# A fused hash-attention and cosine feed-forward kernel: two products issued behind the output copies, one AV step moved, the last tile in two halves, and a new prologue

## The chip, the cores and the metric

The kernel runs on one core of a Trainium2 chip. The metric is device microseconds of one execution, the median over runs; the profile is one such run, and its span is about 1.8 us shorter than that run's time. A ratio is the mean time of one kernel's fast runs over that of the other's of the same rounds, so it is not quite the ratio of the medians quoted beside it. The kernel before is run again beside each group of kernels: its medians were 312.5, 312.7, 312.6, 312.9, 312.9 and 312.4 us, with single runs from 311.8 to 315.4. (The fifth figure is the fourth's runs and one more.)

## The reference

```python
# q, k, v: [4, 8, 768, 64]; proj: [64, 6]; w_in: [512, 2048]; w_out: [2048, 512]
q_bits = (q @ proj > 0);  k_bits = (k @ proj > 0)      # 6 bits per token
mask   = bucket(q_bits)[..., :, None] == bucket(k_bits)[..., None, :]
scores = where(mask, q @ k.T / 8, -1e9)
x      = softmax(scores) @ v                           # -> [3072, 512]
h      = x @ w_in
out    = (h * cos(h)) @ w_out
```

The kernel puts the equality of buckets into the product itself: each token's six hash bits, scaled, are six further rows of q and k, so the score of a matching pair is raised and one exponential with a bias does the rest.

## The kernel before

Four batches of eight heads. The hash matmuls give the bits; the scores, the exponential and the AV product follow per head. When a batch's attention is done, its first feed-forward product (called L1, sixteen blocks of 128 columns with a cosine and a product h\*cos(h) each) runs as one stage in the next batch's attention; the second product (L2) fills PE between scores. There are four L1 stages; the attention stretches between them are called A2, A3 and A4 here. The instruction order on each engine is the program's own.

The L1 block, the output tile of L2 and the loop that joins them:

```python
def l1_ff(b, ff, hp):
    ...                                   # 8 matmuls into hp
    for c_, g_, h_ in pieces:
        nc.scalar.activation(out=c_, in_=h_, func=ACTF.Sin, bias=cos_bias, scale=1.0)
    for c_, g_, h_ in pieces:
        nc.vector.tensor_tensor(out=g_, in0=h_, in1=c_, op=ALU.mult)

def l2_mm():
    ...                                   # one matmul of 512 columns into m_ps
    if ff == NFF - 1:
        ob = obp.tile([P, D_MODEL], FP32, name="ob")
        ...
        if b == B - 1 and qt == T - 1:    # last tile: copied and stored in halves
            ...
        else:
            nc.vector.tensor_copy(out=ob, in_=o_ps)
            nc.sync.dma_start(out=dst, in_=ob)

for ff in range(NFF):                     # one L1 stage
    ...
    l1_ff(bb, ff, hp)
    ...                                   # for batch 0: a mark and loads
    if ff in (0, 1) and len(pend) > 0:
        av_step()
    if bb > 0:
        fill(L1F(ff))                     # L2 matmuls of the batch before
```

From the sixth pair of heads on, POOL issues the three loads of a pair (natq, natk, natv, 384 KB each). SP issues the transposes, and then four small transfers of bit rows per pair:

```python
def bits_dma(pr, js):                     # js = 0..3: q and k of head 0, q and k of head 1
    for j in js:
        dst = (qx(pr), kx(pr))[j % 2]
        nc.sync.dma_start(out=dst[D:KEXT, j // 2, :], in_=bits[pr][...])
```

PE's first score of a head waits for that head's two bit rows.

The softmax here doesn't subtract the row's maximum and nothing guards it: scores larger than these inputs give would overflow.

Of the kernel before, what the change touches and what calls it, by code (L numbers as in the profile page):

```python
# [9 lines left out]
FP32 = mybir.dt.float32  # L10
# [12 lines left out]
def kernel(  # L23
# [29 lines left out]
    NEARLY = 5  # L53

# [23 lines left out]
    wz = glob.tile([P, 512], FP16, name="wz")  # L78
    proj2 = glob.tile([32, 2, NBITS], FP32, name="proj2")
# [12 lines left out]
    state = {"m": 0, "rot": 0, "hold": False}  # L92
# [50 lines left out]
    def blocks(pr, hh=None):  # L143
        if pr not in blk:
            blk[pr] = [blkp.tile([P, 2, T, 2, 32], FP32, name=nm) for nm in ("blkq", "blkk")]
        for w in range(2):
            if hh is None:
                nc.vector.transpose(  # L148
                    out=blk[pr][w].rearrange("p h t c r -> p (h t c r)"),
                    in_=nat[pr][w].rearrange("p h f -> p (h f)"))  # L150
            else:
                nc.vector.transpose(
                    out=blk[pr][w][:, hh].rearrange("p t c r -> p (t c r)"),
                    in_=nat[pr][w][:, hh])
# [158 lines left out]
    def l1_ff(b, ff, hp):  # L313
        halves = hp if isinstance(hp, list) else [hp[:, c, :] for c in range(2)]
        for ft in range(NFT):
            for c in range(2):
                nc.tensor.matmul(  # L317
                    out=halves[c][:, 0:C2],
                    lhsT=win_t[ft][:, ff * P:(ff + 1) * P],
                    rhs=xT[(b, ft)][:, 3 * c:3 * c + 3, :],  # L320
                    start=(ft == 0), stop=(ft == NFT - 1))
        cos = cosp.tile([P, 2, C2], FP16, name="cos")
        g = gp.tile([P, 2, C2], FP16, name="g")
        if isinstance(hp, list):
            pieces = [(cos[:, c], g[:, c], halves[c][:, 0:C2]) for c in range(2)]
        else:
            pieces = [(cos, g, hp[:, :, 0:C2])]
        for c_, g_, h_ in pieces:
            nc.scalar.activation(out=c_, in_=h_, func=ACTF.Sin, bias=cos_bias, scale=1.0)  # L329
        for c_, g_, h_ in pieces:  # L330
            nc.vector.tensor_tensor(out=g_, in0=h_, in1=c_, op=ALU.mult)  # L331
        g_tiles[(b, ff)] = g

# [4 lines left out]

    def l2_mm():
        b, qt, ff = l2q.pop(0)  # L340
        if ff == 0 and not state["hold"]:
            state["m"] = 1 - state["m"]
        o_ps = m_ps[state["m"]]
        g = g_tiles[(b, ff)].rearrange("p c n -> p (c n)")
        nc.tensor.matmul(  # L345
            out=o_ps, lhsT=g[:, qt * P:(qt + 1) * P], rhs=wout_t[ff],
            start=(ff == 0), stop=(ff == NFF - 1))
        if ff == NFF - 1:
            ob = obp.tile([P, D_MODEL], FP32, name="ob")
            dst = out.rearrange("(b p t) n -> b t p n", b=B, t=T)[b, qt]  # L350
            if b == B - 1 and qt == T - 1:
                hw = D_MODEL // 2
                nc.vector.tensor_copy(out=ob[:, 0:hw], in_=o_ps[:, 0:hw])
                nc.sync.dma_start(out=dst[:, 0:hw], in_=ob[:, 0:hw])
                nc.vector.tensor_copy(out=ob[:, hw:], in_=o_ps[:, hw:])
                nc.scalar.dma_start(out=dst[:, hw:], in_=ob[:, hw:])
            else:
                nc.vector.tensor_copy(out=ob, in_=o_ps)  # L358
                nc.sync.dma_start(out=dst, in_=ob)

    def fill(n):
        for i in range(n):
            if l2q and not (state["hold"] and i > 0 and l2q[0][2] == 0):
                l2_mm()
# [17 lines left out]
    def warmup(n):  # L382
        for _ in range(n):
            nc.tensor.matmul(  # L384
                out=s_ps[1][:, 1, :], lhsT=wz[:, 0:P], rhs=wz, start=True, stop=True,
                skip_group_check=True)

    with tc.manual_schedule():
# [3 lines left out]
        nc.scalar.dma_start(out=proj2, in_=proj.rearrange("(c p) i -> p c i", c=2))  # L392
        nc.sync.dma_start(out=nat[0][0][:, 0], in_=aps[0][:, 0])
        nc.scalar.dma_start(out=nat[0][1][:, 0], in_=aps[1][:, 0])
        nc.sync.dma_start(out=nat[0][0][:, 1], in_=aps[0][:, 1])
# [4 lines left out]
        nc.vector.memset(wz, 0.0)  # L400
        nc.vector.memset(exp_bias, EXP_BIAS)
        nc.vector.memset(cos_bias, math.pi / 2.0)
        nc.vector.memset(projblk, 0.0)
# [14 lines left out]
        for b_ in range(4):  # L418
            nc.vector.tensor_copy(
                out=projblk[32 * b_:32 * b_ + 32, :, b_, 0:NBITS], in_=proj2)  # L420
        blocks(0, 0)
# [12 lines left out]
        rows_copy(nc.vector, pe_transposes(0, 0, 1, av_ps[0]))  # L434
        rows_copy(nc.scalar, pe_transposes(0, 0, 0, m_ps[0], range(0, 3)))
        rows_copy(nc.vector, pe_transposes(0, 0, 0, m_ps[1], range(3, 6)))
        blocks(0, 1)
# [66 lines left out]
        for u in range(U):  # L504
# [11 lines left out]
            if u in L1_AT:  # L516
                bb = L1_AT[u]
                state["hold"] = bb > 0
                for ff in range(NFF):
# [7 lines left out]
                    l1_ff(bb, ff, hp)  # L527
                    if bb == 0:
                        nc.gpsimd.tensor_copy(out=mark, in_=g_tiles[(0, ff)][:, 0, 0:1])
# [5 lines left out]
                    if ff in (0, 1) and len(pend) > 0:  # L535
                        av_step()
                    if bb > 0:
# [9 lines left out]
        for ff in range(NFF):  # L547
            hp = (s_ps[0], m_ps, s_ps[1])[ff % 3]
            l1_ff(B - 1, ff, hp)
# [32 lines left out]
```

## Time and profile before

| | before |
|---|---|
| time, median of 3 (range) | 312.45 us (312.0 to 312.58) |
| profiled span | 310.8 us, granted clock 0.999 |
| PE busy | 97% |
| A2, A3, A4 | 45.10, 44.90, 44.51 us |
| L1 stages one to four | 21.19, 25.41, 25.11, 20.80 us |
| end of the fourth stage to the end | 24.66 us |

A stage runs from its first to its last L1 matmul, and A2 to A4 are what lies between. Two lines of the page: the span, and the costliest group that waits for the output copy. A group's columns are line, engine, operation, tiles, count, then busy us and mean ns of one, then the idle time just before it and what ended most of that.

```profile
span 310.8 us, 7680 instructions
...
L345 PE MATMUL m_ps<-wout,g 128*128 128x512 f16 x384 | 109.1, 379 | 2.1 <-DVE ob L358 1.8
```

The view by windows over A2, A3 and A4; the columns are the window, its length, the busy us of PE, weight loads, DVE, ACT and POOL with counts, granted clock, DMA share and GB/s. PE leaves 0.3 us of A2 idle and next to nothing of the other two:

```profile
80.30:125.40 45.10, 44.79 (x523) 27.23 (x521) 37.33 (x90) 42.08 (x50) 28.72 (x41) 1.00 0.70 180
150.81:195.71 44.90, 44.84 (x524) 27.35 (x522) 35.43 (x91) 42.05 (x50) 24.36 (x33) 1.00 0.78 165
220.82:265.33 44.51, 44.51 (x463) 26.08 (x461) 23.57 (x62) 37.15 (x43) 2.89 (x4) 1.00 0.29 74
```

### The profile page before, as it was taken

How to read it: one execution, taken by the hardware profiler on the slowest of the kernel's cores; microseconds unless marked ns; L12 is line 12 of the kernel's file. 1: busy time of each engine (PE TensorE's matmuls, PEld its weight loads, DVE VectorE, ACT ScalarE, POOL GpSimd, SP SyncE). 2: the span in 40 equal slices, each digit the busy share in tenths (PEclk: the TensorE clock that was granted, in tenths of full speed). 3: DMA queues.
4: the chain of work that ended last, by engine and by line, in shares of the span. 5: the costliest groups of instructions: out<-in, count | busy, mean ns of one | idle time of the engine just before them, and what ended most of it. 6: DMA issues, size and time to landing. Idle time of an engine off the chain costs nothing.

```text
span 310.8 us, 7680 instructions
## 1 busy us (share of the span) xinstructions
PE 300.5 (97%) x3074; PEld 181.2 (58%) x3074; DVE 201.5 (65%) x434; ACT 234.1 (75%) x288; POOL 109.1 (35%) x180
## 2 busy tenths in 40 slices
PE   8899999899999999899999999999999999999995
PEld 3577667566566666555566666555566664565442
DVE  3665467877698988756677869757677343477211
ACT  3788999977899999666899999756899993477000
POOL 3897268288484584300064584100030000000000
PEclk9999999999999999999999999999999999999999
DMA  7959959399559976600168988100133222100121
GB/s 213 373 105 187 327 55 216 44 142 179 190 154 253 209 192 152 203 2 0 38 83 235 229 152 194 30 34 0 38 75 90 68 61 86 43 0 0 58 79 69
DMA packets 45332, 37.74 MB, mean 121 GB/s; under 512 B 32264, under 2 KB 39200, under 8 KB 45296
## 3 DMA queue, kind: packets, MB, share of 16 engines
q1 hardware_dynamic: 38080, 19.35, 28.5%
q0 software_dynamic: 6576, 17.17, 21.0%
q10 hardware_dynamic: 640, 0.72, 0.8%
q8 instruction: 24, 0.39, 0.5%
q14 instruction: 12, 0.10, 0.1%
HBM read 27.26 MB, written 6.29 MB: 108 GB/s over the span
## 4 chain that ended last, share of the span: by engine, by line
PE 84%; ACT 9%; DVE 3%; issue 2%; DVEq 0%; ACTq 0%
PE m_ps L345 25%; PE s_ps L317 17%; PE s_ps L249 17%; PE av_ps L275 9%; ACT pt L255 8%; PE m_ps L317 6%; PE m_ps L161 4%; PE av_ps L317 2%; PE s_ps L384 1%; PE m_ps L221 1%; ACT cos L329 1%; DVE ob L358 1%; DVE g L331 1%; DVE blkq L148 1%; PE av_ps L161 1%
## 5 line engine op out<-in xcount | busy, mean ns | idle before, releaser
L255 ACT ACTIVATE pt<-s_ps,exp_bias 128x768 f16<-128x768 f32 x192 | 161.6, 899 | 11.1 <-PE s_ps L249 9.7
L345 PE MATMUL m_ps<-wout,g 128*128 128x512 f16 x384 | 109.1, 379 | 2.1 <-DVE ob L358 1.8
L249 PE MATMUL s_ps<-qx,kx 128*128 128x512 f16 (+1 forms) x384 | 93.8, 326 | 2.6 <-ACT pt L255 1.2
L275 PEld LDWEIGHTS <-pt 128*128 128x128 f16 x1152 | 58.7, 97 | 21.7
L317 PEld LDWEIGHTS <-win 128*128 128x128 f16 x512 | 49.9, 98 | 34.4 <-issue 0.2
L275 PE MATMUL av_ps<-vx,pt 128*128 128x65 f16 x1152 | 65.7, 193 | 0.0
L317 PE MATMUL s_ps<-xT,win 128*128 128x384 f16 x352 | 62.3, 326 | 0.1
L331 DVE TENSOR_TENSOR g<-s_ps,cos 128x768 f16<-128x768 f32 x44 | 42.1, 957 | 29.9 <-ACT cos L329 29.9
L329 ACT ACTIVATE cos<-s_ps,cos_bias 128x768 f16<-128x768 f32 x44 | 39.6, 901 | 27.7 <-PE s_ps L317 26.4
L249 PEld LDWEIGHTS <-kx 128*128 128x128 f16 x384 | 35.2, 97 | 31.1 <-issue 3.3
L345 PEld LDWEIGHTS <-g 128*128 128x128 f16 x384 | 32.8, 98 | 24.4 <-issue 5.7
L135 POOL CAST vx<-natv 128x768 f16<-128x768 f32 x16 | 13.2, 827 | 95.2 <-PE av_ps L275 90.2
L358 DVE COPY ob<-m_ps 128x512 f32<-128x512 f32 x23 | 15.8, 685 | 22.0 <-PE m_ps L345 21.9
L317 PE MATMUL m_ps<-xT,win 128*128 128x384 f16 x120 | 27.6, 326 | 0.0
L329 ACT ACTIVATE cos<-m_ps,cos_bias 128x384 f16<-128x384 f32 x30 | 16.3, 578 | 8.4 <-PE m_ps L317 8.4
L302 DVE TENSOR_TENSOR xn<-tot,rc 128x384 f16<-128x384 f32 x24 | 20.1, 838 | 0.8
L331 DVE TENSOR_TENSOR g<-m_ps,cos 128x384 f16<-128x384 f32 x30 | 15.7, 550 | 2.1 <-ACT cos L329 1.8
L297 DVE COPY dv<-av_ps 128x65 f32<-128x65 f32 x24 | 5.1, 211 | 16.9 <-PE av_ps L275 16.9
L137 POOL TENSOR_TENSOR vhalf<-natv 128x384 f32<-128x384 f32 x16 | 15.9, 995 | 0.0
L130 POOL CAST n16x<-natk 128x768 f16<-128x768 f32 (+1 forms) x16 | 13.0, 810 | 5.8 <-DMA natk<-in_k_dram 5.8
L148 DVE STREAM_TRANSPOSE blkq<-natq 128x768 f32<-128x768 f32 x15 | 14.6, 975 | 0.3
L130 POOL CAST n16x<-natq 128x768 f16<-128x768 f32 (+1 forms) x16 | 13.1, 820 | 4.8 <-DMA natq<-in_q_dram 4.8
(76 smaller groups left out, 267.6 us busy)
## 6 DMA issues: line engine op xcount, KB each, us to landing
out_dram<-ob SPq DMA_DIRECT2D x23, 256.0 KB
natq<-in_q_dram POOLq DMA_DIRECT2D x11, 384.0 KB, 4.1
natk<-in_k_dram POOLq DMA_DIRECT2D x11, 384.0 KB, 4.7
natv<-in_v_dram POOLq DMA_DIRECT2D x11, 384.0 KB, 5.7
win<-in_moe_w_in_dram POOLq DMA_DIRECT2D x4, 512.0 KB, 7.3
wout<-in_moe_w_out_dram POOLq DMA_DIRECT2D x16, 128.0 KB, 4.8
natq<-in_q_dram SPq DMA_DIRECT2D x4, 384.0 KB
natk<-in_k_dram SPq DMA_DIRECT2D x4, 384.0 KB
```

What stands on the lines that cost most here:

```text
L130: engs[w].tensor_copy(out=o_, in_=i_)
L137: nc.gpsimd.tensor_tensor(out=half, in0=nv[:, :, 0:3, :], in1=nv[:, :, 3:6, :], op=ALU.add)
L148: nc.vector.transpose(out=blk[pr][w].rearrange("p h t c r -> p (h t c r)"), in_=nat[pr][w].rearrange("p h f -> p (h f)"))
L249: nc.tensor.matmul(out=sp[:, c, 0:c1 - c0], lhsT=kx(pr)[:, hh, jt * P:(jt + 1) * P], rhs=qx(pr)[:, hh, c0:c1], start=True, stop=True)
L255: nc.scalar.activation(out=pt, in_=sp.rearrange("p c n -> p (c n)")[:, 0:S], func=ACTF.Exp, bias=exp_bias, scale=EXP_SCALE)
L275: nc.tensor.matmul(out=bank[:, qt * W:qt * W + D + 1], lhsT=pt[:, qt * P:(qt + 1) * P], rhs=vx_bufs[pr % 3][:, hh, jt, 0:D + 1], start=Fal ...
L302: nc.vector.tensor_tensor(out=dst, in0=tot[:, :, 0:D], in1=rc.unsqueeze(2).to_broadcast([P, T, D]), op=ALU.mult)
L317: nc.tensor.matmul(out=halves[c][:, 0:C2], lhsT=win_t[ft][:, ff * P:(ff + 1) * P], rhs=xT[(b, ft)][:, 3 * c:3 * c + 3, :], start=(ft == 0) ...
L329: nc.scalar.activation(out=c_, in_=h_, func=ACTF.Sin, bias=cos_bias, scale=1.0)
L331: nc.vector.tensor_tensor(out=g_, in0=h_, in1=c_, op=ALU.mult)
L345: nc.tensor.matmul(out=o_ps, lhsT=g[:, qt * P:(qt + 1) * P], rhs=wout_t[ff], start=(ff == 0), stop=(ff == NFF - 1))
L358: nc.vector.tensor_copy(out=ob, in_=o_ps)
```

## The change

Four things. In the L1 stages of batches 1 and 2, the products of the first two blocks are issued after the L2 matmuls that follow them, so that an output copy does not stand behind a product that waits for a cosine. In stage one, one AV step moves from the second block to the end. The last output tile is computed in two halves of 256 columns, so that the first half's copy lies beside the second half's matmuls. The prologue writes the projection block-diagonally by four transfers, behind the first halves of q and k, and transposes the first k tile ahead of the rest; its warm-up matmuls (which have no use but to keep PE busy before the inputs land) take a constant instead of a tile that is set to zero first.

```diff
-        for c_, g_, h_ in pieces:
-            nc.vector.tensor_tensor(out=g_, in0=h_, in1=c_, op=ALU.mult)
         g_tiles[(b, ff)] = g
+        def products():
+            for c_, g_, h_ in pieces:
+                nc.vector.tensor_tensor(out=g_, in0=h_, in1=c_, op=ALU.mult)
+        return products
...
-                    if ff in (0, 1) and len(pend) > 0:
+                    if ff in AVS[bb > 0] and len(pend) > 0:     # AVS = ((0, 15), (0, 1))
                         av_step()
-                    if bb > 0:
+                    if bb > 0 and ff in GDEF:                   # GDEF = range(2)
                         fill(L1F(ff))
+                        products()
+                    elif bb > 0:
+                        products()
+                        fill(L1F(ff))
...
+    def last_tile():
+        for c, eng in ((0, nc.sync), (1, nc.scalar)):
+            cols = slice(c * hw, c * hw + hw)
+            ...                                  # 16 matmuls of 256 columns
+            nc.vector.tensor_copy(out=ob[:, cols], in_=o_ps[:, 0:hw])
+            eng.dma_start(out=dst[:, cols], in_=ob[:, cols])
...
-        nc.scalar.dma_start(out=proj2, in_=proj.rearrange("(c p) i -> p c i", c=2))
         nc.sync.dma_start(out=nat[0][0][:, 0], in_=aps[0][:, 0])
         nc.scalar.dma_start(out=nat[0][1][:, 0], in_=aps[1][:, 0])
+        for b_, eng in enumerate((nc.scalar, nc.sync, nc.scalar, nc.sync)):
+            eng.dma_start(out=projblk[32 * b_:32 * b_ + 32, :, b_, 0:NBITS],
+                          in_=proj.rearrange("(c p) i -> p c i", c=2))
...
-        rows_copy(nc.vector, pe_transposes(0, 0, 1, av_ps[0]))
+        rows_copy(nc.vector, pe_transposes(0, 0, 1, av_ps[0], range(0, 1)))
         rows_copy(nc.scalar, pe_transposes(0, 0, 0, m_ps[0], range(0, 3)))
         rows_copy(nc.vector, pe_transposes(0, 0, 0, m_ps[1], range(3, 6)))
+        rows_copy(nc.vector, pe_transposes(0, 0, 1, s_ps[1][:, 0, :], range(1, 6)))
```

## The prediction

> **What bounds the kernel now.** I read the page's busy shares first, then the waits, then the chain that ended last by stage, then the timelines around each wait of PE.
>
> ```profile
> PE 300.5 (97%) x3074; PEld 181.2 (58%) x3074; DVE 201.5 (65%) x434; ACT 234.1 (75%) x288; POOL 109.1 (35%) x180
> ...
> PE 84%; ACT 9%; DVE 3%; issue 2%; DVEq 0%; ACTq 0%
> ```
>
> PE is the bound: busy 97% of 310.8 us, and 84% of the chain. Only about 10 us are idle, so a change that leaves PE's work alone can win only what stands in those 10 us, or what pipelined "busy" hides at the start. The view of waits names PE's:
>
> ```profile
> PE m_ps L345 <- DVE ob L358: 1.8, 2, 1.0
> ...
> PE s_ps L384 <- DVE cos_bias L402: 1.2, 1, 1.2
> ...
> PE s_ps L249 <- ACT pt L255: 1.2, 5, 0.3
> ...
> PE s_ps L249 <- DVE qx L232: 0.6, 1, 0.6
> ...
> PE m_ps L345 <- DVE g L331: 0.3, 1, 0.3
> ```
>
> The first row (total, times, longest) is the target of the change's first part. The timeline at the second of the four L1 stages shows the mechanism:
>
> ```profile
> 126.52 1.07 DVE L302 TENSOR_TENSOR xn<-tot,rc 128x384 f16<-128x384 f32 x1
> ...
> 128.42 0.96 DVE L331 TENSOR_TENSOR g<-s_ps,cos 128x768 f16<-128x768 f32 x1 [0.83 <-ACT cos L329]
> ...
> 129.29 0.68 DVE L358 COPY ob<-m_ps 128x512 f32<-128x512 f32 x1
> ...
> 130.03 0.81 PE L345 MATMUL m_ps<-wout,g 128*128 128x512 f16 x3 [1.04 <-DVE ob L358]
> ```
>
> PE finished the output tile's last L2 matmuls by 127.5, but the output copy stands behind product g in DVE's order, g waits for the cosine, and the cosine for an activation-table load (126.19 to 127.47). DVE sits idle 0.83 us in front of g with the copy ready behind it. PE had finished its other work at 128.83 (the six matmuls from 128.65 take 0.18 on the chain) and stood until 130.03.
>
> The prologue's chain, in order of time:
>
> ```profile
> 1.19 3.59 PE s_ps L384 x8
> 4.79 0.46 PE av_ps L161 x2
> ...
> 5.25 0.86 PE av_ps L161 x14
> ...
> 7.35 0.51 PE av_ps L221 x6
> ...
> 7.88 0.56 DVE kx L232
> ```
>
> After it comes the first score at 8.76 (wait of 0.6 for the qx copy) and the first exponential at 9.30; ACT then idles 0.50 before the second, at 10.70. From there to about 58 us ACT is nearly saturated (28.4 of 30 us busy in 28 to 58), so a shift of its start can pass through. From 84 us PE is continuous in the attention stages (41.0 of 41, 41.9 of 42, 43.0 of 43).
>
> **What the Trainium skill says.** "TensorE: Matmul & The Clock Gate", section on the 16 sub-arrays, has ACT and DVE as strict FIFO; the trace agrees: a ready copy waits behind a product that can't start. The same page, "Back-to-back issue gap", gives N/2.4 + 2.5 ns for a warm matmul: 216 ns at N = 512, 109 at 256 (my estimate by it). The trace: 96 matmuls of L345 in 20.73 us are 216 each, and a score pair, 512 and 256, takes 0.33 = 0.216 + 0.109. "DMA: Bandwidth & Descriptors", "Anatomy of one DMA", has about 2 us fixed per transfer (for the other issue path); here the 1.5 KB projection took from issue at 0.73 to its first use at 3.22, so 2.5 us. I use 2.5. "Part 1" of the TensorE page: the clock is halved until some 3.4 us of activity. Here warm-up matmuls take about 0.43 each at the start, twice the 0.216; the hash matmuls at 5.25 still take 0.37 each and those at 9.8 0.25.
>
> **The change part by part.**
>
> *Products behind copies.* In the L1 stages of batches 1 and 2, the product of the first two feed-forward blocks is issued after the L2 matmuls that follow. The instruction order on DVE confirms it: stage two from g, ob, g to ob, g, g; stage three from g, g, ob to g, ob, g. Stage two: the copy can start when xn ends (127.59), so it ends by 128.3, ahead of the cosine's end at 128.38, and g loses nothing. PE is ready at 128.83, finds the bank free, and gains 130.03 - 128.83 = **1.20**. Later blocks need the score bank freed by the first g (129.38, about 131 on PE) and by the second (130.75, about 133): slack. Stage three: PE is ready at 201.26 and the copy ends at 201.95. The tile finished at 199.95, and g0 is over at 199.75, so the copy goes 199.98 to 200.66, and the second product is pushed from 200.38 to 200.70, whose bank is wanted only at 203.6. Gain **0.73**. After both stages PE is continuous, so both reach the end.
>
> *The moved AV step in stage one.* One step of six matmuls (0.18) goes from the second block to after the last. There PE waits today from 80.30 to 80.78 for the last two products of block 14 (chain: cos 77.90, g 78.84 for 1.90, L345 80.78), so the step is hidden in the wait. Everything before is 0.18 earlier; third-block cosine has 0.4 us of ACT idle in front of it. Gain **0.18**.
>
> *Tail.* The last tile's 16 matmuls of 512 become 2 x 16 of 256: 3.49 against 3.46, +0.03 (weights at 30 ns each elsewhere, six AV matmuls in 0.18, so the loads hide). The first half's copy now lies beside the second half's matmuls. Today PE ends 307.03, two copies run to 307.80, the last transfer is issued at 307.84 and the span ends at 310.8. After: one copy of 0.42 behind PE, to 307.51, issue at 307.54. Gain **0.30**.
>
> *Prologue.* Removed: the small load ahead of k's first half, four copies (0.70) and the memset of the warm-up operand. Added: four 64-piece loads of the projection, two on each queue, behind the first halves of q and k. Estimates: warm-up starts near 0.8 instead of 1.19, ends near 4.3 instead of 4.79. The first halves, 196 KB each, now move together; in the slices of the first 3.5 us some 0.2 MB had moved by 2.7, and the rate is then near 380 GB/s, so another 196 KB is 0.5 us more; with the receipt both land about 3.5. Transposes then take 0.49 + 0.54 (from the pair at 8.62 and 9.11): blkk is ready near 4.6 instead of 5.19. The last projection load is issued at 1.66; 1.66 + 2.5 = 4.2, with the queues fuller perhaps 4.6. So the hash starts near 4.6. Sixteen hash matmuls cold are about 1.0 against 0.46 + 0.86 from 4.79: it ends near 5.6 against 6.11, **0.5 earlier** (0.9 if the clock is warm by then).
>
> *First k tile.* Today the first score comes 1.41 after the transposes start (8.76 - 7.35). After: the first k tile, six q tiles (7 x 85 ns = 0.6), qx copy of 0.27 to 0.35, so the score at about 1.0: 0.4 earlier. But the rest of k goes last: its copy of about 0.48 (estimate between 0.35 for 384 columns and 0.56 for 768) ends about 1.53 after the start, where today the pair ends at 1.36. DVE then does the second head's transposes 0.17 later, and those gate the second score. ACT idles 0.50 between first and second exponential, so the first one's earliness is idle time, and I book **-0.17** here. Prologue net: 0.5 - 0.17 = **0.35**.
>
> Second halves and pair 1 load later: four more issues of 0.45, and the issue of k's second half now waits on a semaphore shared with its first half, so about 3.6 instead of 1.66. It landed at 7.73 today, in a full queue, and is wanted by DVE at 9.2; pair 1 is wanted at 11.9 to 14.0. I take this as hidden.
>
> Sum: 1.20 + 0.73 + 0.18 + 0.30 + 0.35 = 2.76. 312.45 - 2.76 = **309.7 us**, a ratio of 0.991.
>
> **The rivals.** (1) *The projection becomes the last input.* Four loads of 24-byte pieces in queues behind 196 KB halves could land at 5 us or later; the hash would not start earlier, and the prologue gives 0 or loses up to 0.8: 310.1 to 310.9. For: DMA is at 0.9 share from 2.5 us on, and k's first half took 3.4 us from issue. Against: these loads stand ahead of the second halves in their queues. (2) *A late load.* k's second half or pair 1, held by the semaphore, comes after DVE wants it; 0.5 to 1 us lost: about 310.5. For: DMA is full until 15 us. Against: 1.5 us slack, and fewer transfers in flight ahead of it. (3) *The L1 gain moves to another wait.* ACT's cosine gates PE instead once the copy is early. Against: per three blocks PE takes 3 x 1.30 plus about one matmul, 4.1 us, where ACT takes 0.90 + 0.90 + 1.05 and DVE 0.96 + 0.96 + 1.03. If half were lost: 310.6. (4) *Warm clock earlier, and the early first exponential counts:* prologue 0.9 or more, 309.0.
>
> **Range and chances.** The L1 and tail terms (2.41) are read from waits that the trace times; I trust them to 0.4. The prologue is open from -0.6 to +1.0. So 308.9 to 310.8. A 2% change needs 6.2 us, twice the sum, and 60% of all PE idle time: faster 0.01, within 2% 0.98, slower 0.01.
>
> **What would show it.** Right: no wait of PE for ob in the waits (1.8 gone), ob ahead of g at the second stage with the copy near 127.6; the L1 stages shorter by 0.18, 1.20 and 0.73; the last copy 0.3 closer to PE's end; first hash matmuls near 4.6 and first exponential near 8.4, with the second only about 0.35 earlier than 10.70. Wrong: PE waits for projblk's transfers at the hash, a DVE wait for natk before blkk, or new idle of PE before L317 or L345 in the L1 stages. The total would be wrong if attention stages change length.

## The result, and the profile after

The changed kernel took 311.01 us (median of 4, 310.61 to 311.34) beside 312.51 us for the kernel before (4 runs); the ratio is 0.9953, with a 95% interval of 0.9934 to 0.9972. It is faster, but the gain is 1.5 us of the 2.76 us predicted, and 311.01 lies just above the range. The page after:

```profile
span 308.8 us, 7712 instructions
...
PE 299.9 (97%) x3090; PEld 182.4 (59%) x3090; DVE 201.3 (65%) x430; ACT 234.4 (76%) x288; POOL 109.1 (35%) x180
...
PE 84%; ACT 6%; DVE 4%; DMA 3%; issue 1%; SPq 0%; DVEq 0%; ACTq 0%
...
L368 PE MATMUL m_ps<-wout,g 128*128 128x512 f16 x368 | 105.6, 379 | 0.1
```

The wait for the output copy is gone: the L2 group's idle time fell from 2.1 to 0.1 us. But the chain has a new member: 3% of DMA, which the chain before did not have. Of its 8.9 us, 3.24 are the first load of q, where the chain now begins, and 5.68 are one transfer of bit rows, kx<-br. The view of waits has it too (total, times, longest):

```profile
PEld L250 <- DMA kx<-br: 1.4, 1, 1.4
PE s_ps L250 <- DMA kx<-br: 1.1, 1, 1.1
PE s_ps L250 <- ACT pt L256: 0.9, 4, 0.3
```

The timeline at the second L1 stage answers to that of before. The copy now starts right behind xn, 0.06 us after the cosine began, and the product follows it:

```profile
126.92 1.07 DVE L303 TENSOR_TENSOR xn<-tot,rc 128x384 f16<-128x384 f32 x1
...
127.88 0.90 ACT L330 ACTIVATE cos<-s_ps,cos_bias 128x768 f16<-128x768 f32 x1
127.94 0.69 DVE L374 COPY ob<-m_ps 128x512 f32<-128x512 f32 x1
128.81 0.96 DVE L335 TENSOR_TENSOR g<-s_ps,cos 128x768 f16<-128x768 f32 x1 [0.18 <-ACT cos L330]
```

The prologue's chain after (start, length, what). The inputs of the hash come at 5.05 instead of 4.6, but its sixteen matmuls take 0.58 us instead of about 1.0, because PE's clock was already warm in this run (the record of the granted clock has full speed from 4.74 us on):

```profile
0.74 3.24 DMA natq<-in_q_dram
...
4.58 0.47 DVE blkk L153
...
5.08 0.58 PE av_ps L162 x16
...
7.81 0.41 DVE kx L233
```

And the same three windows after. A2 is 1.35 us longer than before, and PE stood idle 1.22 us of it instead of 0.31; A3 and A4 are 0.15 longer each:

```profile
79.35:125.80 46.45, 45.23 (x529) 27.48 (x527) 37.36 (x90) 42.26 (x50) 28.77 (x41) 1.00 0.67 173
150.01:195.06 45.05, 44.99 (x524) 27.34 (x522) 35.61 (x91) 42.11 (x50) 24.39 (x33) 1.00 0.80 165
219.27:263.93 44.66, 44.66 (x463) 26.10 (x461) 23.58 (x62) 37.21 (x43) 2.90 (x4) 1.00 0.28 74
```

The spans account for the whole difference. Against before, the second exponential came 0.49 earlier, the stretch from there to stage one was 0.28 shorter, stages one to three were 0.18, 1.20 and 0.90 shorter and the rest behind stage four 0.56; A2, A3 and A4 were 1.35, 0.15 and 0.15 longer. That is 3.61 won and 1.65 lost, 1.96 in all, which is 310.79 - 308.83. So the pieces of the change did what was asked, and the attention stages, which the change does not touch, gave back nearly half.

The wait comes from one place, the third pair of heads in A2. The timeline there, with the transfers that POOL and SP issue, first before (start, length of the issue, engine, line, transfer):

```profile
111.73 1.23 SPq L308 DMA_TRANSPOSE xT<-xn  x1
112.49 0.72 POOL L105 DMA_DIRECT2D natq<-in_q_dram  x1
...
113.07 0.72 SPq L214 DMA_DIRECT2D qx<-br  x1
113.21 0.72 POOL L105 DMA_DIRECT2D natk<-in_k_dram  x1
...
113.83 0.67 SPq L214 DMA_DIRECT2D kx<-br  x1
113.93 0.72 POOL L105 DMA_DIRECT2D natv<-in_v_dram  x1
...
115.04 0.68 SPq L214 DMA_DIRECT2D qx<-br  x1
```

and after:

```profile
110.86 1.23 SPq L309 DMA_TRANSPOSE xT<-xn  x1
...
111.62 0.72 POOL L106 DMA_DIRECT2D natq<-in_q_dram  x1
...
112.34 0.72 POOL L106 DMA_DIRECT2D natk<-in_k_dram  x1
112.61 0.72 SPq L215 DMA_DIRECT2D qx<-br  x1
...
113.06 0.72 POOL L106 DMA_DIRECT2D natv<-in_v_dram  x1
113.40 0.67 SPq L215 DMA_DIRECT2D kx<-br  x1
...
114.20 0.66 SPq L215 DMA_DIRECT2D qx<-br  x1
...
119.11 0.11 PEld L250 LDWEIGHTS <-kx 128*128 128x128 f16 x2 [1.40 <-DMA kx<-br]
```

Look at the gaps between SP's issues. Before, the transpose ends at 112.96 and qx<-br follows 0.11 later; but between the first kx<-br (over at 114.50) and the next qx<-br there are 0.54. After, the gap of 0.52 lies between the transpose (over at 112.09) and the first qx<-br, and the gap behind the first kx<-br is 0.13. Counted in the trace's record of SP's instructions, from 0 as all such numbers here, the pause is ahead of number 79 in both kernels, 0.45 us long, with no semaphore still to come; another stands ahead of number 207. Two more transfers at the start have pushed the loop's instructions past it. On one side of the pause the first head's bit rows go out ahead of natk and natv, on the other behind them.

Not only the order differs. From issue to landing the first kx<-br took 3.82 us before and 5.68 after, and natq, issued at the same place relative to stage one, took 3.64 and 5.27. In between an 8 KB packet of an instruction queue ran. The transfer view of the window from 111 to 119 us has it as a share of sixteen engines, first before, then after:

```profile
q14 instruction: 1, 0.01, 0.2%
```

```profile
q14 instruction: 1, 0.01, 0.9%
```

0.9% of sixteen engines over 8 us is 1.15 us for that one packet (1154 ns in the record); before it took 309 ns and ran 37.4 us after stage one instead of 35.1. The first kx<-br landed before with 1.1 us to spare; after, PE waited 1.1 to 1.4 for it.

The Trainium skill, "Runtime: NRT & Kernel Launch", section "Instruction fetch mechanics", says that each engine's instructions are refilled in blocks, by the engine's own DMA queue, and that crossing a block's border is mostly hidden. "DMA: Bandwidth & Descriptors", section "Queues, rings and completion order", says that each DMA engine goes round its queues packet by packet and that one row of queues is the runtime's own, for refills among other things. The trace agrees with such a row in part: the 8 KB packets are on queue 14, but 24 instruction packets of 16 KB are on queue 8. No run here shows the order in which an engine serves its queues. The trace disagrees with "hidden": 0.45 us on SP, where the first page gives no figure. The pauses at 79 and 207 are 128 instructions apart, and 8192 bytes over 128 are 64 bytes each. That the pause is a block's border is my inference from these numbers; no record names it.

### The profile page after: what moved, and what is told of

It is laid out like the page before. It is cut to its first block, busy times and chain, and to the rows that moved or that the text cites. A ratio compares the mean times of both kernels' runs of the same rounds, so it can differ in the third digit from the quotient of the medians.

```text
span 308.8 us, 7712 instructions
## 1 busy us (share of the span) xinstructions
PE 299.9 (97%) x3090; PEld 182.4 (59%) x3090; DVE 201.3 (65%) x430; ACT 234.4 (76%) x288; POOL 109.1 (35%) x180
## 4 chain that ended last, share of the span: by engine, by line
PE 84%; ACT 6%; DVE 4%; DMA 3%; issue 1%; SPq 0%; DVEq 0%; ACTq 0%
PE m_ps L368 24%; PE s_ps L318 18%; PE s_ps L250 17%; PE av_ps L276 9%; PE m_ps L318 6%; ACT pt L256 6%; PE m_ps L162 4%; PE av_ps L318 2%; DMA kx<-br 2%; PE m_ps L352 1%; DMA natq<-in_q_dram 1%; DVE blkq L149 1%; PE m_ps L222 1%; DVE g L335 1%; ACT cos L330 1%
## 5 line engine op out<-in xcount | busy, mean ns | idle before, releaser
L368 PE MATMUL m_ps<-wout,g 128*128 128x512 f16 x368 | 105.6, 379 | 0.1
L368 PEld LDWEIGHTS <-g 128*128 128x128 f16 x368 | 31.2, 98 | 20.1 <-issue 3.3
```

Of the source, the lines that this page charges most:

```text
L368: nc.tensor.matmul(out=o_ps, lhsT=g[:, qt * P:(qt + 1) * P], rhs=wout_t[ff], start=(ff == 0), stop=(ff == NFF - 1))
```

## The experiments

The theory at the start (theory S) was a systematic loss in A2 through a late transfer; its rival was chance. As parts were undone it became theory P (the prologue brings it) and then theory Q (the position of the pauses in SP's and ACT's programs). Eighteen runs were made, in five groups of four, four, four, four and two, each group on one chip. All gave correct results.

| run | kernel | median us (n) | ratio to before [95%] | A2 | A3 | A4 | end of stage four to the end |
|---|---|---|---|---|---|---|---|
| e1 | the change, again | 311.14 (6) | 0.9947 [0.9905, 0.9989] | 45.97 | 45.05 | 44.66 | 24.11 |
| e2 | before, again | 313.53 (2) | 1.0017 | 45.03 | 44.90 | 44.50 | 24.66 |
| e3 | products alone | 310.26 (6) | 0.9921 [0.9889, 0.9953] | 45.03 | 44.90 | 44.50 | 24.65 |
| e4 | the change, loads earlier | 325.99 (6) | 1.0411 [1.0367, 1.0456] | 46.43 | 52.32 | 44.66 | 24.10 |
| e5 | products, AV, tail | 312.29 (4) | 0.9976 [0.9925, 1.0026] | 45.03 | 44.90 | 44.50 | 24.63 |
| e6 | products, tail, prologue | 312.65 (4) | 0.9980 [0.9923, 1.0036] | 46.09 | 45.06 | 44.67 | 24.11 |
| e7 | products, AV | 310.55 (4) | 0.9935 [0.9873, 0.9997] | 45.03 | 44.90 | 44.50 | 24.66 |
| e8 | prologue alone | 313.39 (4) | 1.0020 [0.9971, 1.0069] | 46.05 | 45.05 | 44.65 | 24.51 |
| e9 | e7 + 2 idle SP loads | 310.70 (4) | 0.9931 [0.9877, 0.9985] | 45.60 | 45.07 | 44.51 | 24.55 |
| e10 | e7 + 1 idle ACT copy | 310.34 (4) | 0.9899 [0.9858, 0.9940] | 45.18 | 45.06 | 44.66 | 24.63 |
| e11 | change + 2 loads + 1 copy | 311.36 (6) | 0.9930 [0.9895, 0.9964] | 45.03 | 44.90 | 44.50 | 25.23 |
| e12 | e5 again | 310.20 (6) | 0.9917 [0.9869, 0.9964] | 45.03 | 44.90 | 44.50 | 24.61 |
| e13 | change + 8 loads + 1 copy | 310.90 (6) | 0.9919 [0.9880, 0.9959] | 45.03 | 44.90 | 44.51 | 24.12 |
| e14 | e13 + 2 warm-up matmuls | 309.48 (6) | 0.9874 [0.9841, 0.9907] | 45.43 | 44.90 | 44.51 | 24.10 |
| e15 | e7 + 1 idle SP load | 309.90 (1) | | 45.06 | 44.90 | 44.50 | 24.51 |
| e16 | e5 + 3 late idle SP loads | 310.07 (6) | 0.9900 [0.9859, 0.9941] | 45.03 | 44.91 | 44.50 | 24.11 |
| e17 | change + 2 warm-up matmuls | 310.71 (5) | 0.9946 [0.9932, 0.9959] | 46.24 | 45.05 | 44.65 | 24.12 |
| e18 | e14 again | 309.45 (4) | 0.9905 [0.9891, 0.9919] | 45.11 | 44.90 | 44.50 | 24.11 |

In every run L1 stage two is 24.21 where the products are deferred and 25.40 to 25.41 where they are not (e4 apart), and stage three 24.21 to 24.22 and 25.11.

### e1 to e4: is it chance, and does an earlier load mend it?

e1 and e2 are the two kernels unchanged. e3 keeps the deferred products alone (the old prologue, tail and AV steps). e4 is the whole change with the loads of the later pairs issued earlier:

```diff
                 cast_qk(n, None, (nc.gpsimd, nc.gpsimd))
+                if NEARLY + 2 <= n < NP - 2:
+                    load(n + 2, nc.gpsimd)
                 blocks(n)
                 cast_v(n)
...
-            elif NEARLY + 1 < n < NP - 1:
+            elif n == NEARLY + 2:
                 at(s0 - 1, lambda n=n: load(n + 1, nc.gpsimd))
```

> The changed kernel, not altered, to see whether its new wait comes back. The profile after has PE waiting 1.1 us for the bit rows of k (kx<-br) near 119 us, a transfer of 5.68 us from issue; the same pair's in the profile before took 3.8 us and nobody waited. Theory S (systematic): the change shifts PE's work against the loads that POOL issues, so the wait recurs at the same pair: PE waits 0.9 to 1.4 us for DMA kx<-br, time 311.0. Theory C (chance): transfer times vary from run to run; the wait is gone or stands at another pair, and the spans of single runs scatter by about 1 us with it.

> The kernel before, not altered, for a second profile of it. Theory S: no wait for DMA kx<-br over 0.3 us. Theory C: a wait for DMA of up to 1 us at some pair is as likely here as in the changed kernel. Time 312.0 to 312.8, the two waits of PE for the output copy again 1.0 and 0.7.

> The kernel before with only the deferred products (old prologue, old tail, old place of the AV step). The gain by the timed waits is 1.20 + 0.73 = 1.93, so 310.5 if nothing takes it back. If the later transfers are what eats the gain, then a wait for kx<-br may show up in the attention stages and the time is 310.5 to 311.5. No wait of PE for ob in the L1 stages in either case.

> The changed kernel with POOL issuing the loads of pairs 9 to 15 before the cast of v of two pairs earlier instead of after it, so some 6 us sooner, ahead of the bit rows instead of beside them. If the bit rows land late because they share the DMA engines with those loads, then the wait for kx<-br goes and the time is 309.2 to 309.9 (1.1 to 1.8 below the changed kernel). If the loads are not the cause, the wait stays and the time is 311.0. If another transfer is then late (loads against the transposes), 310.5 or more with a new DMA wait.

e1 showed the wait in the same place (0.9 us) and A2 at 45.97, so it belongs to the kernel. e2 had no wait for kx<-br, as theory S asks, but its time missed: 313.53 us instead of 312.0 to 312.8, with the second exponential at 12.21 in its profile. e3 had no such wait either, and its 310.26 us was below both runs of the whole change: a part of the change takes back more than it gives. e4 failed. A2 kept its loss, and in the second stage and in A3 the loads now ran beside the DMA transposes of q and k, which landed up to 10.5 us after their issue in A2, where the change has 3.2 to 4.1, and up to 13.0 in A3; PE waited 5.0 us in A3 for DVE's transpose blkq, which came late behind a copy that waited for such a transfer. Moving 384 KB loads to an earlier place only moves the collision.

### e5 to e8: which part?

```diff
e5:  the prologue of before; all else of the change
e6: -    AVS = ((0, 15), (0, 1))
    +    AVS = ((0, 1), (0, 1))
e7:  the prologue and the last tile of before
e8:  the prologue of the change; all else of before
```

> The change with the prologue of the kernel before. The stretch between the first L1 stage and the second (A2) is 45.10 us before, 45.03 with the deferred products alone and 45.97 to 46.45 in the whole change. Theory P (the new prologue brings the late bit rows of A2): A2 stays near 45.1 to 45.2, no PE wait for kx<-br over 0.3, span about 307.6, time about 309.5. Rival A (the moved AV step) or T (the tail's two halves shift what follows): A2 is 46 or more, with the wait for kx<-br, time about 311. Either way stage one 21.01, stage two 24.21, stage three 24.2, and 3.45 us from PE's last start to the end.

> The whole change but with the AV step of stage one back after the second block. Theory P: A2 is 46 to 46.5 with PE waiting about 1 us for kx<-br, stage one 21.19. Theory A: A2 is 45.0 to 45.2, no such wait, time about 309.8. Theory T: as P. The gap of 0.15 per batch (in A2, A3 and A4) stays if the prologue or the tail brings it and goes if the moved AV step does.

> Deferred products and moved AV step, with the prologue and the last tile of the kernel before. Theories P and T: A2 near 45.1, time about 310.1 (0.18 below the deferred products alone). Theory A: A2 46 or more with the wait for kx<-br, time about 311.2.

> The new prologue alone on the kernel before. Theory P: A2 is 46 to 46.5 with a wait for kx<-br of about 1 us, so the time is 312.5 - 0.35 + 1.1 = about 313.2, slower than before. Theories A and T: A2 45.1, time about 312.1. The second exponential comes 0.3 to 0.7 us earlier than in the kernel before of the same batch in both.

A2 is 46.05 and 46.09 in the two with the new prologue and 45.03 in the two without; the 0.15 of A3 and A4 goes the same way. The prologue alone makes the kernel before no faster: 313.39 beside 312.61 us, where 313.2 had been expected. So theory P stands and the AV step and the tail are cleared. One expectation failed: e5's time. For its profiled run (312.14 us) the trace shows why it was high: the first half of k landed only at 5.99 us, so the second exponential came at 12.62 instead of 10.2 to 10.9 in the others with the old prologue (e2, 12.21, apart). In e12 the identical kernel began at 10.24 and had 310.20 us (309.3 to 310.0 expected); the late landing was not the kernel's. e6's median, 312.65, is no better than the kernel before, though its stages are those of the change but for the AV step's 0.19: its profiled run, 310.79, was the fastest of four, and what made the others slower stays open.

### e9 to e12: position or prologue?

The base of e9 and e10 is e7, which has nothing of the new prologue. The loads write a small tile that nothing reads.

```diff
+    pad = glob.tile([1, 2, NBITS], FP32, name="pad")
...
+        for i in range(2):                                                    # e9, e11
+            at(40, lambda i=i: nc.sync.dma_start(out=pad[:, i], in_=proj[0:1, :]))
...
+        for i in range(1):                                                    # e10, e11
+            nc.scalar.copy(out=warm2[:, i:i + 1], in_=exp_bias)
```

> The deferred products and the moved AV step with the old prologue and tail (A2 45.03 in its own run, the pairs after it 44.90 and 44.50), plus two loads of 24 bytes on SP in the first attention stage that nothing reads. In all ten traces SP stands 0.44 to 0.46 us ahead of its 79th recorded instruction, without a semaphore to wait for; old prologue: behind the first head's bit rows of the third group in A2, new prologue (two more SP transfers): ahead of them. Theory Q (the program position of that pause decides): two more SP instructions alone bring it all: qx<-br issued near +33.2 after stage one instead of 32.70, one 8 KB packet of the instruction queue near +34 to +35 lasting over 1 us instead of one near +37.4 lasting 0.3, natq landing 4.8 us or more after issue instead of 3.7, PE waits 0.7 to 1.4 for kx<-br, A2 45.7 to 46.3. The gaps of 0.15 stay away (44.90, 44.50). Rival R (something else in the new prologue, such as its loads' shift of everything in time): A2 stays 45.03.

> The same base, plus one copy of one column on ACT in the prologue that nothing reads, so ACT's program is one instruction longer ahead of the loop, as in the new prologue. Theory Q: ACT's pause at its 193rd, 321st and 449th instruction then falls between a wait and an exponential instead of ahead of the wait, and the three attention stages grow by 0.15 each: A2 45.18, A3 45.05, A4 44.66, and no wait for kx<-br. Rival R: 45.03, 44.90, 44.50.

> The whole change, with the two idle SP loads and the one ACT copy added, which moves SP's pause from the bit rows to ahead of the xT transposes, where SP waits 2.5 us anyway, and gives ACT's program an even shift. Theory Q: A2 back to 45.03 (from 45.97 to 46.45), A3 44.90, A4 44.50, no wait for kx<-br, and the time about 1.2 to 1.6 us below the whole change: 309.4 to 310.0, the fastest of all. Rival R: 311.1 as before.

> The same kernel as in the run that began late (second exponential at 12.62 instead of 10.4 to 10.9, so 312.29): if that late start was chance in the first loads, the stages being 45.03, 24.21, 44.90, 24.22, 44.50, the time is now about 309.3 to 310.0. If it comes again, the old prologue has it in this kernel for a reason, and the time is again near 312.

Two idle loads bring the loss into a kernel with the old prologue. The timeline and the waits of e9 at the same place:

```profile
111.42 1.23 SPq L312 DMA_TRANSPOSE xT<-xn  x1
...
113.18 0.72 SPq L218 DMA_DIRECT2D qx<-br  x1
113.97 0.66 SPq L218 DMA_DIRECT2D kx<-br  x1
...
118.98 0.11 PEld L253 LDWEIGHTS <-kx 128*128 128x128 f16 x2 [0.70 <-DMA kx<-br]
```

The gap of 0.53 is again ahead of the first qx<-br, the instruction packet ran at 34.1 after stage one for 1.25 us, natq took 4.55 us, and A2 grew by 0.57: all in kind as expected, and in size a little below it (natq 4.8 or more, A2 45.7 to 46.3). A3 grew by 0.17, which theory Q had not foretold. The trace shows the path: two DMA transposes (qx<-n16x) landed 6.96 and 6.26 us after their issue, against 6.34 and 5.58 in e7, DVE's blkq and blkk came about 0.7 later behind them, and the hash matmuls 0.17 later. An instruction packet of 2.69 us ran at that time, but that it delayed the transposes is not shown: e13 has one of 1.76 there, and its A3 is 44.90. The two loads also shift the turn of the DMA semaphores by two, which was not tried apart from the position.

The one idle copy on ACT brings the other loss exactly: 45.18, 45.06 and 44.66 were measured, 45.18, 45.05 and 44.66 expected. ACT's own border is ahead of its recorded instruction 191, and the next ones are ahead of 319 and 447; with one instruction more, a pause of 0.32 us lies there between an exponential's wait and the exponential, and the next pair of score matmuls comes 0.15 late. It follows the pair before by 0.73 us in e7 and by 0.88 in e10:

```profile
101.25 0.49 PE L252 MATMUL s_ps<-qx,kx 128*128 128x512 f16 x2
...
101.98 0.49 PE L252 MATMUL s_ps<-qx,kx 128*128 128x512 f16 x2
```

```profile
100.13 0.49 PE L253 MATMUL s_ps<-qx,kx 128*128 128x512 f16 x2
...
101.01 0.48 PE L253 MATMUL s_ps<-qx,kx 128*128 128x512 f16 x2
```

Neither loss shows in the times: e9 and e10 took 310.70 and 310.34 us, e7 310.55 on another chip.

e11, with both, has all three attention stages back at 45.03, 44.90 and 44.50. Theory Q's mechanism stands, but its time did not: 311.36 us instead of 309.4 to 310.0, no better than the change. Something else took the 1.4 us.

### e13 to e16: the end, the start, and what lengthens the transfers

The lengths show one culprit in e11's profile (310.3 us, the fastest of its six runs): the end, 25.23 instead of 24.10. SP closes the program with a row of waits, one after the other, for every DMA semaphore. The view of SP's waits, for the change and for e11:

```profile
SPq L607 <- DMA out_dram<-ob: 1.8, 1, 1.8
```

```profile
SPq L614 <- DMA out_dram<-ob: 3.8, 2, 2.5
```

In the change, the last store's semaphore is the last of the row, and SP has done all others by then. In e11 it comes early in the row: six further waits of 0.06 to 0.08 us follow it, 0.4 in all. And a block's border had been crossed just before; its 8 KB packet ran for 0.76 us beside the store, whose last packet ended 2.85 us after PE's last start instead of 2.17. In the kernel before and in e12 the row has a pause of 0.4 us in it, at SP's number 207. The tail's gain is decided there.

e13 has eight idle loads: two as in e11, and six early in the third L1 stage (at 196 to 198 us in the trace; the expectation says "late in the last attention stage"), which bring the semaphores round to where they were. e16 does the like for e12, with three (at 195 to 196 us). e14 is e13 with ten warm-up matmuls. e15 is e7 with one idle load, to part the order of issue from the packet.

```diff
e13, e14: +   for i, u_ in enumerate((40, 40, 150, 150, 150, 150, 150, 150)):
e16:      +   for i, u_ in enumerate((150, 150, 150)):
e15:      +   for i, u_ in enumerate((40,)):
          +       at(u_, lambda i=i: nc.sync.dma_start(out=pad[:, i], in_=proj[0:1, :]))
e14:      -        warmup(8)
          +        warmup(10)
```

> The whole change with one ACT copy and eight idle SP loads: two in the first attention stage (as in the run with two), six more late in the last attention stage. With two, the attention stages came back to 45.03, 44.90 and 44.50, but PE's last start to the end took 4.58 instead of 3.45: the last store's semaphore came third instead of last in SP's closing list of waits (0.07 each), and an 8 KB instruction packet of 0.76 us ran beside that store (its last packet ended 2.85 after PE's last start instead of 2.17). Eight loads bring the store back to the last wait (semaphores go round by eight) and SP's block border six instructions further ahead of the close. Theory Q: stages 45.03, 44.90, 44.50, end 3.3 to 3.6, span about 307.4 when the first clock is warm (hash matmuls 0.25 each), time 309.2 to 310.2. Rival R: the end is set by chance in the store's landing: 4 or more again.

> As the one before, with ten instead of eight warm-up matmuls, which fill the 0.7 to 1.0 us in which PE waits for its inputs between warm-up and hash in the new prologue. In the traces of the whole change the stretch from the first hash matmul to the second exponential took 5.14 with matmuls of 0.25 each and 6.19 with matmuls of 0.37 each. Theory W: the gap makes the cold starts; without it every start is warm: hash to second exponential 5.1 to 5.3, the runs spread by less than 1 us and the median is 0.3 to 1.0 below the run with eight. Rival: it is chance of the chip, the spread stays as it is, or the two matmuls come cold (0.43 each) and push the hash by 0.2 to 0.3.

> Deferred products and moved AV step with one idle SP load in the first attention stage: the pause is to fall between qx<-br and kx<-br of the first head, so qx<-br keeps its place near 32.70 ahead of the natk load, and only kx<-br falls behind the natv load, near 33.9. It tells two causes of the longer transfers apart. If the instruction packet near +34 does it (it runs beside natq, natk and natv, 1.2 us or more instead of 0.3), natq takes 4.5 or more again and A2 is 45.5 to 46. If it is the order of qx<-br and natk, natq and qx<-br stay at 3.7, and A2 is 45.0 to 45.2.

> Deferred products, moved AV step and the new last tile with the old prologue, plus three idle SP loads late in the last attention stage. They make the last store's semaphore the last in SP's closing waits and put SP's block border ahead of the close. Theory Q: from PE's last start to the end 3.4 to 3.6 instead of 3.95 to 3.98, all else as in that kernel, so about 0.5 faster than its 310.2: 309.4 to 309.9. Rival R: 3.95 again.

The end came as expected in all three: 24.12, 24.10 and 24.11. It is not chance but the place of the last wait and of the border. The times followed less well: e13 had 310.90 us instead of 309.2 to 310.2, and e16 310.07 instead of 309.4 to 309.9, only 0.13 below e12, although its end was 0.50 shorter in the profile.

The start is the other culprit. e13's profiled run began cold, although the prologue is the same as in e11, which began warm. The chain of e1, the first cold one seen, against the change's 0.58 above:

```profile
5.27 0.87 PE av_ps L162 x16
6.13 0.54 PE s_ps L406
```

From the first hash matmul to the second exponential it took 5.14 us in the warm starts (the change, e6, e8, e11) and 6.18 to 6.19 in the cold ones (e1, e4, e13). e13's six runs lay in two heaps, 309.9 to 310.3 and 311.5. The profiled cold run is in the lower one, so the cold clock does not account for the heaps by itself; what else varies in those starts stays open, as only profiled runs can be looked into. With two more warm-ups the gap between warm-up and hash is filled:

```profile
0.78 4.25 PE s_ps L408 x10
...
5.08 0.84 PE av_ps L164 x16
```

(this is e18, the same kernel). e14's six runs lay within 309.31 and 309.93, and the median was 1.4 below e13's, more than the 0.3 to 1.0 expected. The way was not quite theory W's: from hash to second exponential it took 5.40 in e14 and 5.41 in e18, not 5.1 to 5.3, and e17's start below was cold in spite of ten warm-ups. e14's profile was the slowest of the six: PE paused once for 0.48 in stage one and waited 0.5 for kx<-br. That transfer took 5.20 us in e14 and 4.89 in e18, with the pause elsewhere, where the other traces without the pause at that place have 3.7 to 4.3 (e15 apart); so something else can lengthen it too; what it is stays open.

e15 did not part the two causes: the pause fell between qx<-br and kx<-br as planned, but the packet, too, came elsewhere (36.2, 309 ns). In this one profile kx<-br behind natv took 0.5 us more (4.47 against 3.94 in e7), which the slack takes up: A2 45.06. As e18 has 4.89 ahead of natv, this does not price the order.

### e17 and e18: what the positions are worth in time

e17 is the change with ten warm-ups and nothing else; e18 is e14 again.

> The whole change with ten warm-up matmuls and no idle loads. It tells what the position of the pauses is worth when the start no longer varies. Theory Q: the attention stages are again 45.5 to 46.5, 45.05 and 44.66, with PE waiting for kx<-br, and the time is that of the padded kernel with ten (309.48) plus 0.9 to 1.7: 310.4 to 311.2, with a spread under 1 us. Rival: the start was all, the stages' losses do not reach the time, and it is 309.3 to 309.9.

> The fastest kernel again, beside the one without idle loads on the same chip. Theory Q and W: 309.3 to 309.9 with a spread under 1 us, stages 21.0, 45.03, 44.90, 44.50 (the run before had one PE pause of 0.48 in stage one and one wait of 0.5 for kx<-br in its profile, which should not come in each run), 3.45 at the end.

With runs that spread less the stages reach the time: 310.71 (310.60 to 311.17) against 309.45 (308.97 to 309.72), with A2 46.24 against 45.11. The ranges do not touch, and the difference of 1.26 us is what moving two engines' pauses is worth in the change. e17's profiled run was the slowest of its five; it began cold (hash matmuls of 0.37 each, full clock only from 6.74 us), so ten warm-ups do not make every start warm, though the spread is 0.6 to 0.8 us in e14, e17 and e18 against 1.7 in e13 and 3.1 in e1. To the change itself they were worth 0.3 to 0.4 (310.71 against 311.01 and 311.14). A2 of e18:

```profile
79.62:124.73 45.11, 44.98 (x529) 27.48 (x527) 37.31 (x90) 42.08 (x50) 28.72 (x41) 1.00 0.66 178
```

e18 beats both kernels: ratio 0.9905 [0.9891, 0.9919] to before, where the change with the same warm-ups has 0.9946 [0.9932, 0.9959]. e16, the old prologue with mended positions, came to 310.07.

## Why the prediction was right or wrong

| step of the prediction | predicted | measured |
|---|---|---|
| products behind copies, stage two | 1.20 | 1.20 |
| the same, stage three | 0.73 | 0.90 |
| AV step in stage one | 0.18 | 0.18 |
| tail | 0.30 | 0.56 in the change, 0.05 in e12, -0.57 in e11 |
| prologue, second exponential earlier | 0.35 | 0.49 in the change's profile; at 10.2 to 11.5 us in the ten profiles with the new prologue, median 10.50 (old prologue: 10.2 to 12.6, median 10.55) |
| attention stages | not priced | -1.65 in the change's profile, -1.17 in e1's |

**Products.** Right in mechanism and, in stage two, in size: e3 has the 1.20 with nothing else of the change in it. Stage three was worth 0.17 more than the wait read for it.

**AV step.** Right: 21.19 to 21.00 or 21.01 in each run that has it (e14's profile apart), 21.18 to 21.19 in each that does not.

**Tail.** The mechanism was right, the size was not. The step that failed is "one copy of 0.42 behind PE, to 307.51, issue at 307.54", which took the time from the last issue to the end as fixed. It was about 3 us before and 2.7 after, and it depends on where the last store's semaphore stands in SP's closing row and whether a border falls there: the term that read 0.30 measures from -0.57 to 0.56.

**Prologue.** The first half of q landed at 3.98 instead of 3.5, so the hash began at 5.08 instead of near 4.6, later than before. But it ended at 5.66 (predicted near 5.6), because the clock was warm and sixteen matmuls took 0.58 instead of about 1.0: two errors of opposite sign. The first exponential came at 8.40, as predicted. The second came 0.49 earlier, not 0.35. Rival 4 (a warm clock) happened in this run; in e1 it did not, and the second exponential came at 11.45. Rival 1 (the projection as the last input) came true in e6, e8, e11 and e13, where PE waited for projblk and the hash began at 5.26 to 5.37. By the medians in the table the gain at the start is not shown. A term with such a spread should have had a wider range than the one I gave to the sum.

**The total.** This is where it failed, and the step is the prologue's term: "Prologue net: 0.5 - 0.17 = 0.35" (the difference is 0.33), "open from -0.6 to +1.0". What I counted of the new prologue were its transfers' bytes and issue times at the start, not that two more instructions on SP and one on ACT move every later instruction past fixed pauses. Measured, it won 0.49 at the start of the change's profile and lost 1.65 in A2, A3 and A4 (1.17 in e1); alone, in e8, these stages grew by 1.24 and the median by 0.78 (interval of the ratio 0.9971 to 1.0069, so the time alone would not tell). "From 84 us PE is continuous in the attention stages" was right, but PE was continuous in A2 with a slack of 1.1 us in one transfer, and I had not asked which small transfers have how little slack there. My rival 2, a late load, sought it at the start, in the second halves of q and k, where no such wait appeared. The L1 and tail terms that I trusted "to 0.4" came to 2.84 in the profile against 2.41, the surplus being stage three and the tail. The text did name the sign that would tell: "The total would be wrong if attention stages change length." They did. With the positions mended and ten warm-ups the kernel takes 309.45 us beside the 309.7 predicted. That is near, but that kernel has two more warm-up matmuls and nine idle instructions, so it is not the one predicted.

**What is shown and what is not.** Shown: the loss in A2 comes with two more SP instructions (e9), that of 0.15 per stage with one more ACT instruction (e10), and both go when the positions are moved on (e11 and e13 entirely, e18 but for 0.08; e14's profile kept 0.40 in A2, with the wait of 0.5 for kx<-br named above). Six traces have the pause ahead of the first bit rows with the loads at their place (the change, e1, e6, e8, e9, e17). In all six the instruction packet ran from 34.1 to 35.1 us after stage one for 1.15 to 1.68 us, and natq took 4.5 to 5.3; in the others, e4 apart, the packet was elsewhere and natq took 3.5 to 4.2. Argued, not shown: that the packet makes the loads longer and not the other way round. natq is issued ahead of all the others in both orders, so the order alone does not explain it, but no run moved the packet alone. The line between the two groups is thin: 4.5 against 4.2. Open: what delayed the transposes in A3 of e9, what lengthened kx<-br in e14 and e18, and the two heaps of e13.

## What to carry to other kernels

Count the instructions that a change adds to each engine's program, also on engines that seem idle: SP's and ACT's programs paused at fixed counts here (79 and 207; 191, 319 and 447), and two transfers in a prologue can move a pause in front of a small transfer with 1 us of slack a hundred microseconds later. When a stage that a change does not touch grows, compare issue times of the same transfer relative to the stage's start in both traces; then test the position by idle instructions before blaming the change. Narrow the spread of the start before judging differences under 1 us: here two more warm-up matmuls did (1.7 to 0.6 us from e13 to e14).

## What the Trainium skill lacked or had wrong

- "Runtime: NRT & Kernel Launch", "Instruction fetch mechanics", gives blocks of 16 KiB, 256 instructions, for all engines and calls the crossing mostly hidden. Here queue 8 moved 24 packets of 16 KB, which fits PE's 6180 recorded instructions at 256 each, but the 12 packets of queue 14 were 8 KB, the pauses on SP were 128 recorded instructions apart, and each cost 0.36 to 0.45 us of SP's time.
- No page has a price for a refill that runs beside a kernel's own transfers. Here one 8 KB packet took 309 ns in the kernel before and 1154 to 1676 ns where it met three loads, and natq then landed 0.8 to 1.6 us later; which of the two delays the other is not shown.
- No page that I read has the row of waits for the DMA semaphores with which SP closes a program, at about 0.07 us each: the last store's place in it was worth 0.4 us between the change and e11, and a border in it 0.36 to 0.38 us in e12 and the kernel before.
- "TensorE: Matmul & The Clock Gate", Part 1, has a free-running window by which the same kernel starts with more or fewer slow matmuls, and puts the penalty under 1% of a typical span. The runs agree that the same kernel starts differently (the change and e1), and add the price here: 5.14 against 6.19 us from the hash to the second exponential, 0.3% of the span. No run shows that the window is the cause.
